# Six spectrum reads cut into 4 KB pieces in a kernel of spectral mixing and capacity-limited experts

## The chip, the cores and the metric

The kernel runs on one core of a Trainium2 chip. The metric is the device time of one execution in microseconds (us); lower is better. Several executions of the same program are timed and their median is given. One more execution is recorded by the hardware profiler; its span (first to last instruction) is a little shorter than its device time.

The engines, as the profile names them: PE is the matrix engine, with its weight loads shown as PEld; DVE, ACT and POOL are the vector, scalar and general-purpose engines; SP only issues transfers here. Transfers issued by SP run in queue q1, those of ACT in q10, those of POOL in q0, and all of them share 16 DMA engines. A packet is one contiguous run that a DMA engine moves.

## What is computed

The input x is 8 batches of 2496 positions of 256 channels. Each channel is filtered in the frequency domain, and the result goes through a mixture of 8 experts that keep at most 80 positions each:

```python
X = np.fft.rfft(x, axis=1);  y = np.fft.irfft(X * (filt_r + 1j * filt_i), n=2496, axis=1)
tok = y.reshape(8 * 2496, 256);  logits = tok @ w_gate
idx = argmax(logits);  gate = softmax(logits)[idx]
for e in range(8):
    keep = the 80 positions of expert e with the largest gate
    out[keep] = gate[keep] * (relu(tok[keep] @ w1[e]) @ w2[e])      # all other rows are 0
```

At most 640 of the 19,968 rows of the output are not zero, so y itself is needed at 640 positions only.

## The kernel before, in words

**First stage, to about 290 us of the span.** The forward transform is done as a 39-point and a 64-point step on PE (stage1, transpose1, stage2), the filter is multiplied in on DVE and POOL, and turn (L381) turns the filtered spectrum into tiles of 128 partitions. One batch's spectrum is a tile [128, 20, 256] in float32: 128 rows of 20 x 256 x 4 = 20,480 bytes, 2.5 MB. Batches 0 and 1 stay in the core's memory; the others are written by ACT, four of the 20 slices at a time, into the DRAM tiles yf (keep_spectrum, L377). The logits come from the spectra. The zeros of the output are written by SP meanwhile.

**Choice of positions.** DVE and PE find the kept positions (the functions pick_*). The result idxb holds, for each batch, the positions whose y is wanted.

**Second stage, about 290 to 384 us: y at the kept positions.** For batch t this is a matrix product of inverse-transform rows with the spectrum. It needs two inputs:

- fetch(t) (L502) lets POOL gather the rows of the inverse-transform table for the positions in idxb, in two halves of 5,120 bytes a row (L506), into the tile gts. Batches 0 and 1 are fetched near the end of the first stage, batch 2 at about 300 us, batches 3 to 5 from 319.67 us, as soon as DVE has written their positions (L722), and batches 6 and 7 from 343.48 us.
- spectrum(t) (L511) lets SP read yf[t] into the tile yb. There are three buffers, so spectrum(2) is issued at the start and spectrum(t + 3) at the end of batch t (L546), six reads in all, for t = 2 to 7. The write of batch t's result into the DRAM tile y_sel follows it on SP (L547).

PE works in groups of four of the 20 slices. turn_rows (L519) transposes four pieces of gts (L523), ACT copies them to the tile wt (L528), add_rows (L530) multiplies them with four slices of yb and adds the products up in po (L535). The order is written out by hand: `work` holds transposes two groups ahead of the products, `go(n)` runs the next n of them, and the pieces of the choice of positions stand between (L990 to L1033). The two-group lead starts anew at batch NE = 3, where pick_slots(2) (the small products of L791) and gather_gates (POOL gathers of L231) stand before it.

After batch 4, SP also issues the weights of experts 0 and 1 (L224 and L226).

**Third stage, 384 us to the end: the experts.** POOL gathers the chosen rows of y_sel (L1168), PE transposes and multiplies them (L1184 to L1213), and POOL scatters the results to the output.

The same kind of read in spectrum_of (L1097) stands in a branch that is taken only when the choice of positions did not come out; it is not touched.

Of the kernel before, what the change touches and what calls it, by code (L numbers as in the profile page):

```python
# [81 lines left out]
def kernel(  # L82
# [11 lines left out]
    nc = tc.nc  # L94
# [90 lines left out]
    yf = {b: dpool.tile([128, NS, C], F32, name=f"yf_{b}") for b in range(B)}  # L185
# [54 lines left out]
    with ExitStack() as actx:  # L240
# [259 lines left out]
        wts, gts, ybs, pos = {}, {}, {}, {}  # L500
# [10 lines left out]
        def spectrum(t):  # L511
            p = ypool if t % NE < NE - 1 else st["yx"]
            ybs[t] = p.tile([128, NS, C], F32, name=f"yb_{t}", tag="ys")
            nc.sync.dma_start(out=ybs[t], in_=yf[t])

        def weights(e, p, tag):
            load_weights(e, p.tile([128, 2 * NFC * C], F32, name=f"w_{e}", tag=tag))
# [12 lines left out]
        def add_rows(t, g):  # L530
            if g == 0:
                pos[t] = yps.tile([128, 2, 512], F32, name=f"po_{t}", tag="y")
            for i in range(SG):
                s = SG * g + i
                nc.tensor.matmul(pos[t][:, 0, 0:C], lhsT=wts[t, g // 2][:, g % 2, i, :],  # L535
                                 rhs=ybs[t][:, s, :], start=(s == 0), stop=(s == NS - 1))
            if g == NS // SG - 1:
                yr = t2pool.tile([128, 2, C], F32, name=f"yr_{t}", tag="t2")
                if t < B - 1:
                    nc.scalar.copy(out=yr[:, 0, :], in_=pos[t][:, 0, 0:C])  # L540
                else:
                    nc.scalar.copy(out=yr[:, 0, 0:128], in_=pos[t][:, 0, 0:128])
                    nc.vector.tensor_copy(out=yr[:, 0, 128:C], in_=pos[t][:, 0, 128:C])
                st["yr"] = yr[:, 0, :]
                if t < B - 3:
                    spectrum(t + 3)  # L546
                nc.sync.dma_start(out=y_sel[128 * t:128 * t + 128, :], in_=yr[:, 0, :])  # L547
# [276 lines left out]
        with tc.manual_schedule():  # L824
# [3 lines left out]
            for cb in range(NDB):  # L828
                nc.scalar.dma_start(out=gi[:, cb, 128:128 + E],
                                    in_=moe_w_gate[128 * cb:128 * cb + 128, :])  # L830
# [129 lines left out]
            wpool = pool("weights", 2)  # L960
            fp = pool("fp", 2)
            spectrum(2)
            for t in range(NY):
                ybs[t] = ysb[t]
# [663 lines left out]
```

## Time and profile before

| | us |
|---|---|
| median of 8 runs | 454.34 |
| lowest and highest of the 8 | 453.19, 455.62 |
| the profiled execution | 453.48 |
| its span | 451.6 |
| PE busy | 432.3 (96% of the span) |
| PE busy between 300 and 320 us | 20.00 |
| PE busy between 320 and 330 us | 8.64 |
| PE busy between 340 and 380 us | 40.00 |

The profiled execution lies 0.86 us under the median, near the fast end of the runs; 1.9 us of it lie outside the span. The share of busy time is taken per engine; PE and PEld overlap. In a row of the timeline the first two numbers are the start and the length, and the bracket at its end is the idle time before it with the engine or transfer that ended it. The view of a window's DMA gives, for each queue, packets, megabytes and the time the packets took as a share of 16 engines over that window.

### The profile page before, as it was taken

How to read it: one execution, taken by the hardware profiler on the slowest of the kernel's cores; microseconds unless marked ns; L12 is line 12 of the kernel's file. 1: busy time of each engine (PE TensorE's matmuls, PEld its weight loads, DVE VectorE, ACT ScalarE, POOL GpSimd, SP SyncE). 2: the span in 40 equal slices, each digit the busy share in tenths (PEclk: the TensorE clock that was granted, in tenths of full speed). 3: DMA queues.
4: the chain of work that ended last, by engine and by line, in shares of the span. 5: the costliest groups of instructions: out<-in, count | busy, mean ns of one | idle time of the engine just before them, and what ended most of it. 6: DMA issues, size and time to landing. Idle time of an engine off the chain costs nothing. (4 is left out here: it accounts for less than half of the span.)

```text
span 451.6 us, 8686 instructions
## 1 busy us (share of the span) xinstructions
PE 432.3 (96%) x3369; PEld 407.1 (90%) x3369; DVE 194.1 (43%) x580; ACT 217.0 (48%) x362; POOL 180.2 (40%) x249
## 2 busy tenths in 40 slices
PE   7699999999999999999999999999989999999992
PEld 5689999999999999999999998888878888898881
DVE  2455554444674444664544789658320000111010
ACT  3447766666666666677666754432222332111110
POOL 8548633433444543454453454420555002122201
PEclk9979999999999999999999999999999999999998
DMA  7726545799887887888994132697898991899500
GB/s 209 238 63 204 166 115 148 257 362 375 313 249 244 302 289 242 268 265 248 334 399 183 71 119 94 232 389 296 327 348 303 371 374 53 293 369 372 170 11 20
DMA packets 40091, 109.36 MB, mean 242 GB/s; under 512 B 5336, under 2 KB 16158, under 8 KB 39272
## 3 DMA queue, kind: packets, MB, share of 16 engines
q1 hardware_dynamic: 29078, 75.81, 49.5%
q10 hardware_dynamic: 6466, 21.05, 11.9%
q0 software_dynamic: 4496, 11.85, 8.0%
q8 instruction: 29, 0.48, 0.4%
q14 instruction: 22, 0.18, 0.1%
HBM read 68.37 MB, written 43.20 MB: 247 GB/s over the span
## 5 line engine op out<-in xcount | busy, mean ns | idle before, releaser
L373 POOL TENSOR_TENSOR p<-p,p 128x256 f32<-128x256 f32 x154 | 110.1, 737 | 135.3 <-DVE p L366 88.6
L366 DVE TENSOR_TENSOR p<-pb,ft 128x512 f32<-128x512 f32 x160 | 102.2, 680 | 12.2 <-PE pb L358 12.1
L332 ACT COPY t<-pa 128x480 f32<-128x480 f32 (+1 forms) x84 | 81.0, 970 | 26.6 <-PE pa L325 25.5
L325 PE MATMUL pa<-wf_t,x 117*128 117x120 f32 x684 | 89.7, 278 | 3.6 <-DMA x<-in_x_dram 2.8
L386 PE MATMUL py<-gi,p 128*128 128x136 f32 x640 | 87.8, 280 | 1.3 <-POOL p L373 0.7
L325 PEld LDWEIGHTS pa<-wf_t,x 117*128 117x128 f32 x684 | 83.5, 193 | 5.2 <-DMA x<-in_x_dram 1.8
L358 PE MATMUL pb<-d_t,t 128*128 128x128 f32 x640 | 86.2, 278 | 0.4 <-ACT t L349 0.2
L386 PEld LDWEIGHTS py<-gi,p 128*128 128x128 f32 x640 | 79.8, 190 | 1.7 <-POOL p L373 1.0
L358 PEld LDWEIGHTS pb<-d_t,t 128*128 128x128 f32 x640 | 78.9, 193 | 1.5 <-ACT t L349 0.5
L349 ACT COPY t<-pt 128x512 f32<-128x512 f32 x80 | 46.8, 585 | 61.0 <-PE pt L347 59.2
L535 PE MATMUL po<-yb,wt 128*128 128x256 f32 x240 | 56.6, 380 | 1.3 <-ACT wt L528 1.3
L347 PE MATMUL pt<-ident,t 128*128 128x128 f32 x320 | 49.2, 278 | 2.7 <-issue 2.7
L535 PEld LDWEIGHTS po<-yb,wt 128*128 128x128 f32 x240 | 43.4, 190 | 6.3 <-ACT wt L528 1.5
L409 DVE COPY z<-py 128x16 f32<-128x16 f32 x60 | 11.2, 187 | 84.2 <-ACT ysp L402 56.0
L528 ACT COPY wt<-pw 128x512 f32<-128x512 f32 x39 | 22.7, 585 | 49.5 <-PE pw L523 41.5
L347 PEld LDWEIGHTS pt<-ident,t 128*128 128x128 f32 x320 | 38.7, 144 | 2.9 <-issue 2.9
L402 ACT COPY ysp<-py 128x512 f32<-128x512 f32 x60 | 35.4, 591 | 1.0 <-PE py L386 1.0
L1198 PEld LDWEIGHTS ph<-xs,w 128*128 128x128 f32 x256 | 29.6, 192 | 0.6
L1198 PE MATMUL ph<-xs,w 128*128 128x80 f32 x256 | 29.5, 274 | 0.0
L1213 PE MATMUL po<-w,hT 128*80 128x256 f32 x128 | 28.8, 379 | 0.0
L1213 PEld LDWEIGHTS po<-w,hT 128*80 128x80 f32 x128 | 18.6, 150 | 7.5
L506 POOL DMA_INDIRECT gts<-rows_tbl,idxb x16 | 16.1, 1008 | 21.0 <-DVE idxb L722 16.7
(207 smaller groups left out, 328.8 us busy)
## 6 DMA issues: line engine op xcount, KB each, us to landing
out_dram<-zero_t SPq DMA_DIRECT2D x64, 312.0 KB
x<-in_x_dram SPq DMA_DIRECT2D x40, 468.0 KB
w<-in_moe_w_dram SPq DMA_DIRECT2D x16, 1024.0 KB
yf<-ysp ACTq DMA_DIRECT2D x30, 512.0 KB
yb<-yf SPq DMA_DIRECT2D x6, 2560.0 KB
yf<-ys ACTq DMA_DIRECT2D x10, 512.0 KB
x<-in_x_dram SPq DMA_DIRECT2D x11, 117.0 KB
d_t<-d_tbl SPq DMA_DIRECT2D x5, 256.0 KB
```

The lines of the kernel that those rows point to most:

```text
L325: nc.tensor.matmul(out=ps[:, i, :, 2 * NS * cb:2 * NS * cb + 2 * NS], lhsT=xt[0:NJ * N1, (2 * k + i) % JC, 128 * cb:128 * cb + 128], rhs=w ...
L332: copy(out=t1[:, 2 * k:2 * k + full], in_=ps[:, 0:full])
L347: nc.tensor.transpose(ps[:, i, cb, :], t1[:, a:a + 2, :].rearrange("p r n -> p (r n)"), ident[:])
L349: nc.scalar.copy(out=t2[:].rearrange("p i c -> p (i c)"), in_=ps[:].rearrange("p i c q -> p (i c q)"))
L358: nc.tensor.matmul(out=ps[:, cb, i], rhs=d_t[:, 2 * u + i, :], start=True, stop=True, lhsT=t2[:, i, 128 * cb:128 * cb + 128])
L366: nc.vector.tensor_tensor(out=pt, in0=ps[:].rearrange("p c s r q -> p (c s) r q"), in1=f.unsqueeze(2).to_broadcast([128, 2 * NDB, 2, NQ]), ...
L373: adder.tensor_tensor(out=yt[:, :, r, :], in0=yt[:, :, r, :], in1=pr[1][:, :, 1 - r, :], op=op)
L386: nc.tensor.matmul(out=ps[:, i, ZW * cb:ZW * cb + ZW], rhs=gi[:, cb, :], lhsT=yt[:, 2 * cb + i].rearrange("p r q -> p (r q)"), start=True, ...
L402: nc.scalar.copy(out=dst.rearrange("p s (h w) -> p s h w", h=2), in_=pv[:, :, :, 0:128])
L535: nc.tensor.matmul(pos[t][:, 0, 0:C], lhsT=wts[t, g // 2][:, g % 2, i, :], rhs=ybs[t][:, s, :], start=(s == 0), stop=(s == NS - 1))
L1198: nc.tensor.matmul(ph[:, fc // 4, fc % 4, 0:cap], lhsT=self.w1s[e][:, k, 128 * fc:128 * fc + 128], rhs=xs[:, k, :], start=(k == 0), stop=( ...
L1213: nc.tensor.matmul(po[0:cap, :], lhsT=hT[:, fc, :], rhs=self.w2s[e][:, fc, :], start=(fc == 0), stop=(fc == NFC - 1))
```

## The change

One argument is added to the read in spectrum(t). It limits the contiguous run that one piece of the transfer covers to 4,096 bytes, so a row of 20,480 bytes is given out as five pieces, and a read as 640 pieces in place of 128. The bytes, their places, the issuing engine, the order and the waits stay as they are.

```diff
         def spectrum(t):
             p = ypool if t % NE < NE - 1 else st["yx"]
             ybs[t] = p.tile([128, NS, C], F32, name=f"yb_{t}", tag="ys")
-            nc.sync.dma_start(out=ybs[t], in_=yf[t])
+            nc.sync.dma_start(out=ybs[t], in_=yf[t], max_dma_last_dim=4096)
```

## The prediction

> **What bounds the kernel now.** I read four views: the page's first part, the waits of PE in the second stage, the DMA of single windows, and the timeline at the one place where PE stops. The page first:
>
> ```profile
> PE 432.3 (96%) x3369; PEld 407.1 (90%) x3369; DVE 194.1 (43%) x580; ACT 217.0 (48%) x362; POOL 180.2 (40%) x249
> yb<-yf SPq DMA_DIRECT2D x6, 2560.0 KB
> ```
>
> PE is the bound, and the change touches six transfers. So the question is where PE waits for a transfer in the stretch in which they run, 285 to 385 us. The waits of PE there (engine, line, what ended the wait; us, times, longest):
>
> ```profile
> PE po L535 <- ACT wt L528: 1.3, 1, 1.3
> PE py L386 <- issue: 0.6, 1, 0.6
> PE po L535 <- DVE wt L528: 0.4, 1, 0.4
> PE px L1186 <- ACT yr L542: 0.2, 1, 0.2
> PE pw L523 <- issue: 0.2, 1, 0.2
> ```
>
> No line says that PE waited for yb. The trace puts the ends of the last packets of the six reads at 303.0, 313.7, 325.7, 338.6, 350.4 and 363.0 us, and the first products that use them (L535) at 316.4, 330.2, 341.2, 352.0, 362.9 and 373.7 us. Each read is 10.7 to 16.5 us early. Two waits of that list stand together, and a gather of POOL is near them. The timeline of PE, then of POOL:
>
> ```profile
> 326.82 0.75 PE L791 MATMUL misc<-eval__1_3701,eplc 128*80 128x32 bf16 x16
> 327.79 1.06 PE L523 MATMUL pw<-ident,gts 128*128 128x128 f32 x8 [0.22 <-issue]
> 330.16 1.13 PE L535 MATMUL po<-yb,wt 128*128 128x256 f32 x4 [1.30 <-ACT wt L528]
> ```
>
> ```profile
> 319.67 0.99 POOL L506 DMA_INDIRECT gts<-rows_tbl,idxb  x1 [16.74 <-DVE idxb L722]
> 320.96 0.99 POOL L506 DMA_INDIRECT gts<-rows_tbl,idxb  x1 [0.30 <-issue]
> ```
>
> L523 at 327.79 is the first transpose of batch 3. It reads the first half of gts, gathered from 319.67. The trace's last recorded arrival of that gather is 327.29, and PE's queue passes its wait for it at 327.68, 0.11 us ahead of the transpose; it passed the same wait 2.8 us ahead for batch 2 (311.36, transposes from 314.14) and 3.1 us ahead for batch 4 (335.45, 338.60). So for batch 3 the queue was held until the gather landed. Why did it take 7.6 us? The DMA of the window 317 to 323, then of 324 to 327:
>
> ```profile
> q1 hardware_dynamic: 109, 2.23, 100.2%
> q8 instruction: 1, 0.02, 1.0%
> ```
>
> ```profile
> q0 software_dynamic: 301, 0.78, 71.4%
> q1 hardware_dynamic: 157, 0.19, 17.4%
> ```
>
> While q1 moved 20 KB packets of spectrum(4), POOL's queue q0 moved none; from 323.9 us, with that read nearly done, it moved 301 packets in 3 us.
>
> **The change part by part.**
>
> *The bytes.* The trace's packets of q1 take 761 ns (median) at 20,480 bytes and 159 ns at 4,096. Five pieces are 795 ns: 34 ns more a row, 8 rows a DMA engine, 0.27 us a read. It is hidden by the 10.7 us or more by which each read is early; without that cover the last read would cost PE 0.27 us once.
>
> A rule speaks against the change. The Trainium skill, "DMA: Bandwidth & Descriptors", section "Why small descriptors are slow (HBM only)", charges every packet about three bus cycles and every descriptor 32 bytes of extra traffic. Four more descriptors a row are 128 bytes, an estimate of 0.6%, where the two rows above give 4.5%; by the page the read grows by about 0.04 us instead of 0.27, hidden alike.
>
> *SP.* L514 takes SP 0.32 us. The weight reads show issue without a full queue: 0.384 us for 256 rows (L224's shortest), 0.462 for 1024 (L226's shortest). 640 pieces lie between: about 0.42, so 0.1 us more, six times. SP waits before these issues (47.6 us in four waits on PE), so its own time is free. Queued behind each issue is the write of y_sel (L547), needed from 376.43 us on, and after the last one the weights (L224, L226), used from 385.8 us.
>
> *Who gets the DMA engines.* This is the part that can reach PE. How q0 fares beside 4 KB pieces of q1 is not in the trace. The nearest row is the stretch 225 to 237 us, where SP had zero writes of 2,496 bytes queued back to back while ACT wrote spectra:
>
> ```profile
> q1 hardware_dynamic: 1676, 3.72, 81.1%
> q10 hardware_dynamic: 288, 1.05, 21.7%
> ```
>
> There ACT's write issued at 230.88 moves its first packets from 232 and 58 packets between 233 and 234, beside 66 of q1: the newcomer has its share within about 2 us, though q1 is full. Beside 20 KB packets the gather issued at 319.67 got its first packet 4.2 us later, and the one at 343.48 waited 4.5. The bounds for the gather of batch 3: as late as now (pieces queue just as deep), or about 2 us to the first packet and an even share, which lands the half near 325, some 2.5 us before PE needs it. I take the second: 4,096 bytes are nearer to 2,496 than to 20,480.
>
> [...]
>
> *What that is worth.* Three terms. First, the idle 0.28 us of PEld (0.22 of PE) before 327.79 goes: L791's last weight load ends at 327.47 and nothing else is late. Second, the 1.30 us at 330.16. It waits for ACT's copy of the new transposes, and that copy began 1.10 us after the transposes' recorded end at 328.42; 37 of the stage's 40 such copies begin within 0.24 us of theirs. The signal from PE came late, and the profile does not say why. Bounds: 0, if it has nothing to do with transfers, as another late copy (0.96 us at 340.16, no gather due) suggests; 1.1, if it hangs on the gather. I take half, 0.55. What is late next: ACT's copy (0.58 us) against the second group of transposes, about 0.2 us that stays. Third, the profiled execution (453.48) is 0.86 us faster than the median. A gather that lands just in time here lands late in a run whose transfers run a little later, and then PE waits one for one. Bounds 0 and 0.86; I take a third, 0.3.
>
> Sum: 0.28 + 0.55 = 0.83 against the profiled execution (453.48 to 452.65), and 0.83 + 0.3 = 1.1 against the median: 454.34 - 1.1 = 453.2. About 0.2%, 0.9 us, is what a measurement of this kernel can tell from no change, so this is a small gain.
>
> The other gathers have room: batch 2's packets end by 308, for transposes from 314; batch 4's by 331, for 339; batch 5's by 341, for 349; those of 6 and 7 by 357 but for some four packets, for 360 and 371. Their coming sooner is worth nothing.
>
> **The rivals.**
>
> *Nothing to measure.* Either pieces starve the gather as rows do, or the wait is only the 0.28 us seen and the late signal stays. For it: PE is busy 20.00 of 20 us from 300 to 320 and 40.00 of 40 from 340 to 380; the pool of time to win is small. 454.34 less 0 to 0.3 gives 454.1, with the scatter of medians 453.5 to 455.2. That the argument doesn't cut the rows to 4 KB at all (it might count elements) ends here too.
>
> *Slower, at the hand-over to the experts.* From 351.79 SP queues spectrum(7), y_sel of batch 4, four weight transfers, y_sel of batches 5 and 6. The timeline of SP shows the queue full:
>
> ```profile
> 351.79 0.32 SPq L514 DMA_DIRECT2D yb<-yf  x1
> ...
> 354.02 6.97 SPq L224 DMA_DIRECT2D w<-in_moe_w_dram  x1
> 361.03 2.74 SPq L226 DMA_DIRECT2D w<-in_moe_w_dram  x1
> ```
>
> The queue empties at about 375, and y_sel of batch 6, issued at 373.85, is behind it. POOL's gathers of the experts wait for it (376.43); the first lands at 378.8 and PE uses it at 383.43: 4.6 us of room. If pieces made spectrum(7) take twice its 11 us (issue to landing), the queue would end some 11 us later and PE would stop for about 6. At 1.3 times that it is nothing; it decides from 1.4 times on. Price 1 to 3 us for a moderate case: 455.3 to 457.3. Against it: the two packet rows say 1.05 times, not 1.4. A spectrum read that is itself late needs the same factor of two.
>
> **How the numbers follow.** Faster, 0.44: 453.2, from 452.1 (0.28 + 1.1 + 0.86 = 2.2 us gone) to 453.4. Same, 0.38: 454.1, 453.5 to 455.2. Slower, 0.18: 455.3 to 457.3; the share is more than the rows give, since the late signals show that something on PE moves by a microsecond for reasons the profile does not name, and a new packet pattern could move it either way. The range runs from 452.1 to 455.6, the slowest run of before; it leaves out most of the slower case and what lies under 452.1, under 0.2 together. Faster and same hold most of the chance; the faster case's own range is 452.1 to 453.4.
>
> **What will show it.** The DMA of 317 to 323 us has q0 packets; the gather of batch 3 lands before 326; the 0.22 us before the transposes of batch 3 are gone and the 1.30 us behind them shrink; q1 has no packet of 20 KB; each read of yb still lands 8 us or more before its use; y_sel of batch 6 still goes out near 374. The prediction is wrong if the gather lands early and PE still reaches batch 3's products 2.5 us after L791's last product (then the late signal is not the gather's), if q0 still stands still beside the pieces, or if a wait for yb, w or xg appears on PE.

## The result, and the profile after

The changed kernel takes 460.32 us (median of 17 runs, 457.63 to 462.61); the kernel before, in the same comparison, 454.22 us (46 runs). The ratio is 1.0136, 95% interval 1.0119 to 1.0154: slower by 1.4%. I had forecast 453.2 us, with a range to 455.6.

The profiled execution of the changed kernel took 456.51 us (span 454.7), less than any of its timed runs and 3.03 us more than that of before. The page, at the places shown for before:

```profile
PE 434.6 (96%) x3369; PEld 408.0 (90%) x3369; DVE 193.4 (43%) x580; ACT 217.0 (48%) x362; POOL 180.2 (40%) x249
yb<-yf SPq DMA_DIRECT2D x6, 2560.0 KB
```

The instructions are the same. The trace's 768 packets of 20,480 bytes are now 3,840 of 4,096, with a median of 159 ns. Where does PE stop? Its waits between 285 and 390 us:

```profile
PE po L535 <- ACT wt L528: 2.4, 3, 1.2
PE po L535 <- issue: 0.9, 1, 0.9
PE pw L523 <- issue: 0.8, 1, 0.8
```

Nobody waits for yb. PE waits for ACT's copies of the transposes, three times instead of once. First the place that the prediction was about, PE at the start of batch 3, and the transfers of 317 to 323 us:

```profile
326.49 0.75 PE L791 MATMUL misc<-eval__1_3701,eplc 128*80 128x32 bf16 x16
328.02 1.07 PE L523 MATMUL pw<-ident,gts 128*128 128x128 f32 x8 [0.78 <-issue]
329.84 1.99 PE L535 MATMUL po<-yb,wt 128*128 128x256 f32 x8 [0.75 <-ACT wt L528]
```

```profile
q1 hardware_dynamic: 524, 2.15, 94.3%
q8 instruction: 1, 0.02, 1.1%
```

The two waits are 0.78 + 0.75 = 1.53 us where they were 0.22 + 1.30 = 1.52. Nothing is gained: the rows of the second view have no q0 packet, as before.

The loss is in batch 4. Up to there the changed kernel is 0.3 us ahead (first products of batches 2 and 3 at 316.08 and 329.84 us, before 316.42 and 330.16). One group of products follows the other after 2.17 us in the steady state; the steps to the first, second and third group of batch 4 (at 341.93, 344.83 and 348.48 us) are 3.21, 2.90 and 3.65 us, which is 3.25 us too much and, less the 0.3 us, close to the whole difference of the spans. PE, then ACT, in that stretch:

```profile
338.28 0.60 PE L523 MATMUL pw<-ident,gts 128*128 128x128 f32 x4
338.71 1.89 PE L535 MATMUL po<-yb,wt 128*128 128x256 f32 x8
340.44 0.60 PE L523 MATMUL pw<-ident,gts 128*128 128x128 f32 x4
341.93 1.99 PE L535 MATMUL po<-yb,wt 128*128 128x256 f32 x8 [0.88 <-issue]
343.76 0.60 PE L523 MATMUL pw<-ident,gts 128*128 128x128 f32 x4
344.83 1.99 PE L535 MATMUL po<-yb,wt 128*128 128x256 f32 x8 [0.47 <-ACT wt L528]
```

```profile
336.64 0.58 ACT L528 COPY wt<-pw 128x512 f32<-128x512 f32 x1 [1.58 <-issue]
341.29 0.58 ACT L528 COPY wt<-pw 128x512 f32<-128x512 f32 x1 [4.06 <-PE pw L523]
...
344.19 0.59 ACT L528 COPY wt<-pw 128x512 f32<-128x512 f32 x1 [1.10 <-remote]
347.84 0.59 ACT L528 COPY wt<-pw 128x512 f32<-128x512 f32 x1 [3.07 <-PE pw L523]
```

The transposes at 338.28 end by the record at 338.88. ACT sits idle and copies them at 341.29, 2.41 us later; the normal distance is 0.03 to 0.09 us. PE's products of 341.93 begin 0.05 us after that copy (the row says "issue", but the copy is what they waited for). The next two copies are 3.15 and 3.49 us late, a fourth 1.34. So PE's signal to ACT comes late, the copy with it, and PE waits for the copy. The Trainium skill, "Perfetto Trace Analysis", section "Tensor Engine Instruction (MATMUL, LD_WEIGHTS)", says that a matmul's recorded end is an estimate and that the signal is sent only when the result's memory has acknowledged it. The rows agree that the two can come apart, by up to 3.49 us here. The trace also records the updates of the semaphore that these copies wait for: they stand at 341.21, 344.17, 347.77 and 348.58 us, at most 0.08 us ahead of the copies and 1.3 to 3.4 us behind the recorded ends, where the normal distance is about 0.01. So it is PE's signal that is late and not ACT; whether the product itself ended late or only its signal, the trace does not show. The granted clock is no rival here: it is 1.00 throughout 285 to 384 us of this execution.

What else runs at that time? POOL, before and after:

```profile
336.52 0.95 POOL L231 DMA_INDIRECT gate<-gates,idxt  x1 [0.30 <-issue]
337.98 0.94 POOL L231 DMA_INDIRECT gate<-gates,idxt  x1 [0.51 <-issue]
340.58 0.94 POOL L231 DMA_INDIRECT gate<-gates,idxt  x1 [1.66 <-DMA gts<-rows_tbl,idxb]
342.23 0.95 POOL L231 DMA_INDIRECT gate<-gates,idxt  x1 [0.70 <-DMA gate<-gates,idxt]
```

```profile
336.20 0.95 POOL L231 DMA_INDIRECT gate<-gates,idxt  x1 [0.30 <-issue]
337.45 0.94 POOL L231 DMA_INDIRECT gate<-gates,idxt  x1 [0.30 <-issue]
338.70 0.95 POOL L231 DMA_INDIRECT gate<-gates,idxt  x1 [0.30 <-issue]
340.97 0.94 POOL L231 DMA_INDIRECT gate<-gates,idxt  x1 [1.32 <-issue]
```

Before, POOL issued six gathers in a row from 331.48 us and then had to wait for earlier row gathers to land (1.66 us), and once more (0.70). After, it issues seven in a row, pauses 1.32 us and issues five more. The trace's waits say what each pause hangs on. POOL's gathers take eight semaphores in turn, so each waits for the gather eight before it: before, the seventh of this row waits for the first half of batch 5's rows, issued at 326.25; after, that half has landed in time, and the eighth waits for the second half, issued at 327.21. The row gathers land sooner beside pieces. This is the DMA of 331 to 337 us, before and then after:

```profile
q1 hardware_dynamic: 153, 2.13, 82.9%
q0 software_dynamic: 160, 0.27, 11.8%
```

```profile
q1 hardware_dynamic: 456, 1.70, 70.4%
q0 software_dynamic: 264, 0.70, 29.8%
```

Once both queues run, q0 moves 2.6 times the bytes beside pieces, and the packet of its last row starts at 339.8 us instead of 341.3.

### The profile page after: what moved, and what is told of

Its sections match the earlier page's. It is cut to its first block, busy times and chain, and to the rows that moved or that the text cites. A ratio compares the mean times of both kernels' runs of the same rounds, so it can differ in the third digit from the quotient of the medians.

```text
span 454.7 us, 8686 instructions
## 1 busy us (share of the span) xinstructions
PE 434.6 (96%) x3369; PEld 408.0 (90%) x3369; DVE 193.4 (43%) x580; ACT 217.0 (48%) x362; POOL 180.2 (40%) x249
## 5 line engine op out<-in xcount | busy, mean ns | idle before, releaser
L325 PE MATMUL pa<-wf_t,x 117*128 117x120 f32 x684 | 91.7, 281 | 2.2 <-DMA x<-in_x_dram 1.3
L325 PEld LDWEIGHTS pa<-wf_t,x 117*128 117x128 f32 x684 | 85.2, 197 | 4.4 <-DMA x<-in_x_dram 1.6
L347 PE MATMUL pt<-ident,t 128*128 128x128 f32 x320 | 48.1, 273 | 2.2 <-issue 2.2
L523 PE MATMUL pw<-ident,gts 128*128 128x128 f32 x160 | 23.8, 273 | 0.8 <-issue 0.8
```

What stands on the lines that cost most here:

```text
L325: nc.tensor.matmul(out=ps[:, i, :, 2 * NS * cb:2 * NS * cb + 2 * NS], lhsT=xt[0:NJ * N1, (2 * k + i) % JC, 128 * cb:128 * cb + 128], rhs=w ...
L347: nc.tensor.transpose(ps[:, i, cb, :], t1[:, a:a + 2, :].rearrange("p r n -> p (r n)"), ident[:])
```

## The experiments

The runs fell on several chips, and they come in two kinds: chips where the kernel before takes about 454 us (the result above is from such a one, and so are again2, only5b, but5b, g_late, b_late, p10b, paced2 and b_twice2), and chips where it takes about 449. I call them 454 and 449 chips. Each set of runs after the first fell on a chip of its own, so the chip and the session are not told apart here. The two kinds differ early: the transposes of the second stage begin at 288.9 to 291.7 us in the kept traces of the first kind and at 285.1 to 287.9 in those of the second, so most of the 5 us is there before any late signal. "Late" is the time from the recorded end of four transposes to the start of ACT's copy.

**Undo and halve the change, on a 449 chip.** The changed kernel again; pieces for batch 5's read alone, the one in flight from 326.7 us, into batch 4; pieces for all but that one; pieces of 10 KB. The edit, each in place of L514's call:

```diff
# again
+            nc.sync.dma_start(out=ybs[t], in_=yf[t], max_dma_last_dim=4096)
# only5 (but5: t != 5)
+            nc.sync.dma_start(out=ybs[t], in_=yf[t], **(dict(max_dma_last_dim=4096) if t == 5 else dict()))
# p10
+            nc.sync.dma_start(out=ybs[t], in_=yf[t], max_dma_last_dim=10240)
```

> The changed kernel once more, for a second profile. Both theories: 1.3 to 1.4% slower than before. Theory A (the loss is made in the products of batch 4, where ACT's copies of the transposes began 1.3 to 3.5 us late in the first profile) expects late copies there again, 3 to 6 us lost between the first products of batches 4 and 5, and steps of 10.8 us between the other batches. Theory B (each read in pieces costs a little) expects the loss spread over batches 2 to 7, about 1 us each.

> Only the read for batch 5 goes in 4 KB pieces, the other five in rows. That read is the one in flight when the copies of batch 4 come late. Theory A: most of the loss, +1.0 to +1.4% against before. Theory B: a sixth of it, about +0.2%.

> All reads but that for batch 5 go in 4 KB pieces. Theory A: 0 to +0.3% against before. Theory B: five sixths of the loss, about +1.1%. A loss in full would say that another read makes it, first of all that for batch 4 or 6.

> All six reads in two pieces of 10 KB a row. If the loss comes from the share that the gathers get beside smaller pieces, it lies between the two kernels, +0.3 to +1.0%. If it comes from the number of descriptors alone, 256 in place of 640 a read give about a quarter of the loss, +0.3%.

Measured, beside 448.82 us for before: 0.9998 [0.9973, 1.0023], 0.9994 [0.9969, 1.0020], 0.9999 [0.9978, 1.0020] and 0.9995 [0.9969, 1.0020]. Whatever was expected of a loss was missed: the change does nothing here. In again no copy of the stage is over 0.3 us late. The change costs time only where PE's signals come late, and these runs can't say why.

**The same on a 454 chip.** The changed kernel, and pieces for batch 5's read alone.

> The changed kernel once more, in another session. In the first session it and the kernel before took the same time, 449.4 and 448.8 us, and no copy of ACT came late; in the runs of the result they took 460.3 and 454.2. Theory C (the loss needs a state of the chip in which PE's completion signals come late, and the kernel before then also takes some 454 us): where the kernel before takes 453 us or more here, this one is 1.0 to 1.5% slower and its profile shows late copies in batch 4; where it takes under 451 us, the two are the same. Theory B (the pieces themselves cost time): 1.3% slower in either state.

> Only the read for batch 5 in pieces. Where the kernel before takes 453 us or more: +1.0 to +1.4% if the loss hangs on that read alone, about +0.2% if each read makes its share. Where it takes under 451 us: 0.

Measured, beside 453.82 us: again2 1.0124 [1.0062, 1.0186], only5b 1.0156 [1.0079, 1.0232]. In again2 the first four copies of batch 4 are 2.42, 3.17, 4.23 and 1.79 us late; in only5b the latest is 5.83. The result repeats, and this one read is enough for a loss of that size.

**The other reads, and the gathers of gates moved.** For g_late and b_late (the changed kernel and the kernel before) gather_gates goes behind the last row gathers on POOL:

```diff
             pick_slots(2)
-            gather_gates()
             go(8)
             pick_slots(4)
             go(next(i for i, w in enumerate(work) if w[:2] == ("m", B - 1)))
+            gather_gates()
```

> All reads in 4 KB pieces but that for batch 5, which keeps its rows. If the kernel before takes 453 us or more in these runs, this chip shows the loss. Theory C (the loss comes from the one read that is under way together with the gathers of the gates): ratio 1.000 to 1.004, no wait of over 1 us behind batch 4's product groups. Theory D (pieces of any read cost some time, batch 5's only most of it): 1.005 to 1.010. Where the kernel before takes under 451 us, both say 1.000.

> The changed kernel, with the eight gathers of gates put behind the last four gathers of rows on POOL, so that they run at about 347 to 357 us in place of 331 to 341. If the kernel before takes 453 us or more: Theory C1 (gate gathers and the pieces of batch 5's read together make PE's signals late) gives at most 1.004 and copies of batch 4's transposes that begin within 1 us of their end; Theory C2 (the pieces beside the gathers of rows are enough, the gates have no part) gives 1.010 to 1.016 with copies 2 us late or more in batch 4. A third way: the late signals move with the gates to the stretch from 347 on, beside the read for batch 7, with the same loss there. Where the kernel before takes under 451 us, all say 1.000.

> The kernel before, with the gathers of gates moved in the same way: what the move alone is worth. Theory C1: the 0.96 us by which the first copy of batch 4 is late goes, 0.997 to 1.001. Theory C2: 1.000. If the signals are late wherever the gates run: 1.000 to 1.005 and a late copy past 347 us.

> All reads in pieces of 10 KB, two a row. If the kernel before takes 453 us or more: if the number of packets sets the lateness, 1.000 to 1.005 (a tenth of the added packets of 4 KB would be 0.1%, but the share that the gathers get lies between); if any cut of the rows is enough, 1.010 or more. Under 451 us: 1.000.

Measured on a 454 chip (before 454.29 us): but5b 0.9993 [0.9966, 1.0019], g_late 1.0147 [1.0105, 1.0188], b_late 1.0049 [1.0023, 1.0075], p10b 1.0011 [0.9979, 1.0042]. The five other reads in pieces cost nothing, and pieces of 10 KB cost nothing. The surprise is b_late: every read in rows, no instruction added, and it is slower. ACT in its profiled execution:

```profile
346.77 0.59 ACT L528 COPY wt<-pw 128x512 f32<-128x512 f32 x1 [2.45 <-PE pw L523]
351.00 0.58 ACT L528 COPY wt<-pw 128x512 f32<-128x512 f32 x1 [3.65 <-PE pw L523]
355.36 1.07 ACT L528 COPY wt<-pw 128x512 f32<-128x512 f32 x2 [3.77 <-PE pw L523]
```

These copies are 0.91, 2.98, 5.17 and 1.77 us late, from 346 us on, while POOL issues ten gathers without a pause from 339.52. (This execution, 459.62 us, is the slowest of its ten; the fastest took 454.32, so the loss varies from run to run.) In g_late the late copies moved in the same way, to 344 to 356 us. So the lateness follows POOL's gathers and does not need pieces. That gave Theory E: on these chips PE's signals are late when POOL issues many gathers in a row. Theory F was that pieces beside gathers make them late.

**Pauses with pieces, and more gathers with rows.** paced keeps the 4 KB pieces and gives POOL three clears of an idle tile (1.7 us) after every second gather of gates; b_paced is the same with rows; best adds a pause ahead of batch 5's row gathers; b_twice keeps the rows and issues the gathers of gates a second time, so it has eight gathers more.

```diff
# paced, b_paced, best
+    rest = lambda: nc.gpsimd.memset(kt[:], 0.0)
...
         for e in range(E):
+            [rest() for _ in range(3 * (e in (2, 4, 6)))]
# best, best_p
+            rest(), rest(), rest(), fetch(NE + 2)
# b_twice (without the clear of gate the second time)
-                            fetch(7)
+                            fetch(7), gather_gates(False)
```

> The changed kernel (all reads in 4 KB pieces), with three clears of an idle tile on POOL (about 0.54 us each by the clear of kt at the start) behind every second of the eight gathers of gates, so that POOL never issues more than four gathers in a row in batch 4. If the kernel before takes 453 us or more: Theory E (PE's signals are late when POOL issues seven or more gathers without a pause; the pieces only take away the pauses that POOL used to make for gathers that had not landed) says 1.000 to 1.004 and no copy of batch 4 over 1.2 us late. Theory F (the pieces beside the gathers make the signals late) says 1.010 to 1.016 as before. Where the kernel before takes under 451 us, both say 1.000.

> The kernel before (rows of 20 KB) with the same clears between its gathers of gates: the control. Theory E: 0.997 to 1.002, and the copy of batch 4 that began 0.96 us late begins on time. Theory F: 1.000.

> The kernel before with those clears, and three clears between the gathers of rows for batch 4 and those for batch 5, which follow each other at 323 to 328 us. If the kernel before takes 453 us or more: Theory E says that the copies of batch 3, which begin about 1.1 us late, begin on time, 0.995 to 0.999 (1.1 to 1.3 of 454 us at best). Theory F: 1.000. Under 451 us: 1.000.

> The kernel before (rows of 20 KB) with the eight gathers of gates issued a second time, behind the last gathers of rows, so at about 348 to 358 us (work that is added; it writes the same values again). If the kernel before takes 453 us or more: Theory E says late copies in batches 4 and 5 and 1.004 to 1.012; Theory F, by which only pieces of a read do this, says 1.000. Under 451 us: 1.000.

They met a 449 chip (before 448.94 us): 1.0004 [0.9987, 1.0020], 1.0002 [0.9987, 1.0016], 1.0003 [0.9985, 1.0020] and 1.0012 [0.9996, 1.0027], with no copy over 0.3 us late. As tests of the theories they are inconclusive; but b_twice has twelve gathers in a row there, nothing is late, and the added work costs at most 0.3%. So gathers in a row are not enough by themselves: what tells the two kinds of chip apart has a part too.

> The changed kernel with clears of an idle tile on POOL behind every second gather of gates, as in the run paced. If the kernel before takes 453 us or more: Theory E (POOL's gathers without a pause make PE's signals late) says 1.000 to 1.004 and no copy of batch 4 over 1.2 us late; Theory F (the pieces beside the gathers) says 1.010 to 1.016. Under 451 us: both 1.000.

> The kernel before (rows of 20 KB) with the eight gathers of gates issued a second time at about 348 to 358 us, as in the run b_twice (work that is added). If the kernel before takes 453 us or more: Theory E says late copies in batches 4 and 5 and 1.004 to 1.012; Theory F says 1.000. Under 451 us: 1.000 to 1.003, as measured there.

These two met a 454 chip (before 454.15 us): paced2 1.0028 [0.9995, 1.0062], b_twice2 1.0185 [1.0136, 1.0233]. POOL in paced2:

```profile
334.31 0.95 POOL L231 DMA_INDIRECT gate<-gates,idxt  x1 [0.21 <-issue]
335.57 0.95 POOL L231 DMA_INDIRECT gate<-gates,idxt  x1 [0.30 <-issue]
336.52 1.70 POOL L239 MEMSET kt<- 128x512 f32 x3
338.43 0.95 POOL L231 DMA_INDIRECT gate<-gates,idxt  x1 [0.21 <-issue]
```

ACT in b_twice2:

```profile
350.51 0.58 ACT L528 COPY wt<-pw 128x512 f32<-128x512 f32 x1 [1.75 <-PE pw L523]
354.05 0.59 ACT L528 COPY wt<-pw 128x512 f32<-128x512 f32 x1 [2.95 <-issue]
359.01 0.37 ACT L540 COPY yr<-po 128x256 f32<-128x256 f32 x1 [4.37 <-remote]
361.14 0.58 ACT L528 COPY wt<-pw 128x512 f32<-128x512 f32 x1 [1.76 <-remote]
```

With the pieces kept and POOL made to pause, batch 4 has no late copy and Theory F's 1.010 lies outside the interval. With rows and eight gathers more, three copies of batch 5 are 1.58, 6.50 and 4.88 us late, and the loss is larger than the change's own, and than Theory E's 1.004 to 1.012. Theory F falls; Theory E has the sign of both, though not the size of the second. The control with rows and pauses, b_paced, ran on a 449 chip alone.

The 454 chips side by side. "In a row" means less than 0.6 us between two gathers of POOL:

| kernel | reads | POOL's gathers in a row, from | late copies (over 0.5 us) behind the first two of batch 3 | ratio |
|---|---|---|---|---|
| but5b | batch 5 in rows | 5, 333.01 | none | 0.9993 |
| before | rows | 6, 331.48 | 0.96 | 1 |
| p10b | 10 KB | 6, 331.35 | 0.98 | 1.0011 |
| paced2 | 4 KB | 2, 2, 2, then 6, 342.55 | 0.61 | 1.0028 |
| after | 4 KB | 7, 331.15; 5, 340.97 | 2.41, 3.15, 3.49, 1.34 | 1.0136 |
| only5b | batch 5 in 4 KB | 7, 332.14; 5, 341.45 | 1.43, 3.56, 5.83, 1.90 | 1.0156 |
| b_late | rows | 10, 339.52 | 0.91, 2.98, 5.17, 1.77 | 1.0049 |
| g_late | 4 KB | 11, 338.18 | 0.93, 3.01, 6.61, 3.18 | 1.0147 |
| b_twice2 | rows | 11, 343.38 | 1.58, 6.50, 4.88 | 1.0185 |

Up to six in a row, no copy of the table is a microsecond late; from seven on, the latest of each run is 3.5 to 6.6 us late. The step from six to seven is read from few profiles, one of the gaps that I count as none is 0.51 us (before, ahead of 337.98), and the pause behind the row (1.66 us before, 1.32 after) may matter as much. It is not the whole rule either: the first two copies of batch 3, left out of the table, are 0.55 to 1.15 us late in every one of these runs, behind two gathers, a pause, and four more.

**A version that might beat both.** In the kernel before, the late copies of batch 3 (1.10 us) follow two plus four row gathers, so a pause among them might save up to 1.3 us on a 454 chip. best2 is best once more, and best_p the same with the pieces.

> The kernel before (rows of 20 KB) with three clears of an idle tile on POOL between the gathers of rows for batches 4 and 5, and behind every second gather of gates. If the kernel before takes 453 us or more: Theory E says the copies of batch 3 begin within 0.5 us of their transposes' end and the time is 0.995 to 0.999 of before. If the late copies of batch 3 hang on the gather that lands late and not on POOL's gathers in a row, 1.000. Under 451 us: 1.000.

> The same with all reads in 4 KB pieces. If the kernel before takes 453 us or more: Theory E says 0.995 to 1.002 (paced, which lacks the pause ahead of batch 5's gathers, took 1.0028 [0.9995, 1.0062]). Theory F: 1.010 or more. Under 451 us: 1.000.

Both met a 449 chip (before 448.83 us): 1.0001 [0.9983, 1.0018] and 1.0004 [0.9989, 1.0020]. Whether they gain on a 454 chip stays open; no run here is measurably faster than the kernel before.

## Why the prediction was wrong

**The packets, SP and the reads' own lateness: right.** Pieces take 159 ns, L514 takes SP 0.36 us (forecast 0.42), and the first four reads land at 303.7, 315.1, 327.0 and 341.8 us, 12 us or more ahead of their use. The fourth lands 3.2 us later than before, having lost its share to q0, and that is hidden too. The estimate by the skill's page, 0.6%, was short by that page itself: it counts the 32 bytes of each descriptor and leaves out the bus cycles of each packet that the sentence ahead of it names. Nothing else rests on it.

**Who gets the DMA engines: the step that failed first.** I took the bound "about 2 us to the first packet and an even share" for the gather of batch 3, because 4,096 bytes are nearer to the 2,496 of the row used. The trace has no q0 packet from 317 to 323 us; the first comes at 323.5, 4.1 us after the issue (before: 4.3). The other bound, "as late as now", was the true one. The row used was a write of ACT's queue beside writes of SP's, not a gather of POOL's beside a read. A nearer row stood in the trace of before, at the gathers for the experts, with the DMA from that issue to the gather's first packet:

```profile
386.98 0.94 POOL L1168 DMA_INDIRECT xg<-y_sel,idxg  x1 [7.08 <-DMA y_sel<-yr]
q1 hardware_dynamic: 898, 1.61, 99.9%
```

Beside the weights' packets, 1.8 KB in the mean, this gather of POOL too had to wait, 4.30 us, where the one of 376.43, with q1 idle, waited 1.66. Smaller packets in q1 had not made it sooner.

**What that is worth: 0.28 + 0.55 came out as 0.** The trace's record of the gather's arrivals is incomplete, but PE's queue passes its wait for the gather at 327.92 us, not near 325 and 8.6 us after the issue, where it had been 327.68 and 8.0. So the first idle time grew from 0.22 to 0.78 us and the second shrank from 1.30 to 0.75: together still 1.5. The third term, 0.3 us for the slower runs, went with them; no profile of such a run was kept, so nothing shows it by itself.

**The late signal: the step that cost the sign.** I gave the 1.10-us late copy a bound of 0 "if it has nothing to do with transfers", and read the second one (0.96 us at 340.16, "no gather due") as a point against the gathers. Both in fact follow six gathers issued by POOL, two from 319.67 and four from 323.62 us, and six from 331.48; POOL's timeline showed it, but I looked at what PE waits for, and not at what POOL was issuing. The terms had no price above zero for this signal. The runs put it at 3.25 us in the profile of after, and at 1.85% of the time in b_twice2.

**The rivals.** "Pieces starve the gather as rows do" was right in its mechanism, and on the 449 chips in its time (0.9998). The slower rival named the hand-over to the experts; y_sel of batch 6 goes out at 376.90 us, 3.05 later than before, as late as PE itself, so the hand-over added nothing. The slower case that came true (batch 5's gathers land sooner, POOL no longer pauses, PE's signals come late) was in none of my cases; only the remark that the late signals "could move it either way" touched it.

**How far the cause is shown.** Shown: the loss on 454 chips is that of batch 5's read alone (only5b, but5b); in the profile of after it stands in late copies; the lateness follows POOL's gathers when they move (g_late, b_late) or grow (b_twice2), without pieces; pauses of POOL take it away with pieces (paced2); and with pieces POOL's pause goes because batch 5's rows have landed (the waits of before and after). Only argued: that it is this pause, one gather later and 0.3 us shorter, that decides, and not another effect of the rows landing together with the gates. Open: why a signal of PE is late beside POOL's gathers (their issue, their small packets or their own completions would each look the same here), and why only on some chips. The medians lose 6.1 us where the profiled execution loses 3.0; that the rest is more of the same is likely from again2 (4.23 us late) but not shown. The clock may have a part in it: the profile of only5b has two steps of 3.4 us at half clock, from 331.0 and from 351.5 us, worth up to 1.7 us each by my estimate (half of 3.4, with PE busy throughout), and that of after has none there. Among the timed runs of after, the two of 457.6 us had a mean granted clock of 0.991 and 0.993, the five of 461.9 us and more 0.983 to 0.985 (the mean counts steps anywhere in the run).

## What to carry to other kernels

When a transfer gets out of the way of another, ask what the engine that issues the other one does next: a wait that vanishes there can be what kept two things apart (the last step of this is argued here, not shown). A late start that the profile puts down to an engine long done is a term with its own price, above zero as well as below; look at what every other engine was issuing in the microseconds before it. And where a signal is late at all, time the kernel on more than one chip, since the same change cost 1.4% on one and nothing on another.

## What the runs showed of the hardware that I had not expected

- A POOL gather that comes while q1 is busy got its first packet 4.1 us after its issue beside 4 KB pieces, 4.3 us beside 20 KB rows and 4.3 us beside the weights' smaller packets; with q1 idle it took 1.66 us. Once started, q0 moved 0.70 MB in 6 us beside pieces and 0.27 beside rows. The Trainium skill, "DMA: Bandwidth & Descriptors", section "Queues, rings and completion order", has each DMA engine take turns between its queues, but only after a whole packet of typically 9 to 17 descriptors; what the profile calls a packet is one run, so these rows neither confirm nor contradict it.
- Chips (or sessions) differ: the kernel before took 453.8 to 454.3 us in four sets of runs and 448.8 to 448.9 in three, and late signals stand only in traces of the first kind, though b_twice has twelve gathers in a row on a 449 chip.
- After a stop of PE the granted clock can fall for some microseconds, but it need not: in again2 PE was busy 2.05 of the 4 us from 348, and the next 4 us kept a clock of 1.00. In only5b PE was busy 1.93 of 4 us, and the next 4 us had a clock of 0.64; the columns are the window, its length, PE's and the other engines' busy time, then the clock, the DMA share and GB/s:

```profile
348.00:352.00 4.00, 1.93 (x9) 1.53 (x8) 0.00 (x0) 1.35 (x3) 0.00 (x0) 0.93 0.97 283
352.00:356.00 4.00, 4.00 (x16) 3.24 (x15) 0.00 (x0) 0.58 (x1) 0.00 (x0) 0.64 1.02 411
```
